# A second TensorE loop, and an earlier start of the first, in a one-core attention decode kernel

## The chip, the cores and the metric

One core of one Trainium2 chip runs the whole kernel. The metric is device time in microseconds (us), the median of several executions. The record marks all runs reported here as fast.

## The reference, cut to what matters

Two attention decode steps (one query per sequence, batch 4, 32 heads of 128) are computed and put side by side. Part A is a sliding window: 8 key/value heads, of whose cache only the last 2048 positions count. Part B is full: 32 heads, 8192 positions.

```python
# A: W = 2048, keys and values repeated 4 times over the query heads
q = (x @ wq) per head;  s = q . k[:, :, -W:] * Dh**-0.5;  o = softmax(s) . v[:, :, -W:];  a = o @ wo
# B: the same with all 8192 positions and no repetition
return concatenate([a, b], axis=-1)
```

587 MB are read once (587.21 MB in the trace of before, at 426 GB/s over the span, with the DMA engines over 90% busy in all but the last of its forty slices): this is a kernel of memory traffic.

## The kernel before

The work is cut into *chunks*. A has 8 (one key/value head, all four sequences; 2 MB of keys and 2 MB of values). B has 128 (two heads of one sequence; 4 MB and 4 MB); I number them 8 to 135. For each chunk TensorE transposes the keys in groups of 8 tiles into PSUM; VectorE and ScalarE copy the groups out (`kt`), TensorE multiplies them with the query (`sc`), the other engines do the softmax, and TensorE multiplies the values (`po`) one chunk later, between the groups of the next.

```python
def keys_part(c):                        # transposes of chunk c, scores two groups behind
    if c >= NCA and (c - NCA) % 2 == 0:
        sch.mark()                       # a loop round may start here: pairs of B chunks only
    for g in range(ch["NG"]):
        emit_T(ch["s"] + g)
        if g >= SLAG: emit_S(ch["s"] + g - SLAG)
        ...                              # statistics of chunk c-1, in A also its exp and sums
for c in range(NC):
    keys_part(c)
    ...
    values_part(c - 1 if c else None, c) # values of chunk c-1, last scores and row maxima of c
```

A recording layer keeps each engine's instructions with the semaphore counts that they wait for. `periods` finds the longest stretch that repeats with constant steps, and only that becomes a hardware loop; the rest is written out. Before, the loops of TensorE, VectorE and ScalarE run from the second pair of B (chunk 10) to the end.

SBUF holds ten half-slots of 2 MB. B uses two slots of two halves each for keys and two for values. A key slot is free when the chunk's last transpose is done, a value slot when its `po` product is done; only then does the SP queue issue the next load into it, strictly in order (in the trace of after B's first keys go out at 112.02 us, behind output weights that waited for their slot until 111.05).

```python
HALF_A = {"k": (2, 3, 8, 0, 1), "v": (6, 7, 9, 4, 5)}     # A: five half-slots each
at = HALF_A[kind][c % 5] if ch["ab"] == 0 else (0 if kind == "k" else 4) + 2 * (c % 2)
waits = take((kind, c), at, ..., ("T", ch["s_last"]) if kind == "k" else ("pv", c))
```

Of the kernel before, what the change touches and what calls it, by code (L numbers as in the profile page):

```python
# [12 lines left out]
P = 128  # L13
# [4 lines left out]
NWO = 3  # L18
# [25 lines left out]
class _Sched:  # L44
# [39 lines left out]
    def emit_ops(self, ops, eng, sems, step=None, count=None):  # L84

        waited = {}
        for k, (emit, waits, sig, at) in enumerate(ops):
            for sname, val in self.needs(waits).items():
                if waited.get(sname, 0) >= val:
                    continue  # L90
                by = step[sname] if step else 0
                eng.wait_ge(sems[sname], count * by + val if by else val)
                waited[sname] = val
            if at is None:
                ins = emit(eng)
            else:
                ins = emit(eng, count * step[k] if step else 0)
            if sig is not None:
                ins.then_inc(sems[sig[0]], sig[1])
# [4 lines left out]
    def periods(self, engname, pairs):  # L104


        ops, marks = self.ops[engname], [m[engname] for m in self.marks]
        rec = _Record()
        says = [(emit(rec) if at is None else emit(rec, -at), sig) for emit, _, sig, at in ops]
        best = (0, 0, {})  # L110
        for a in range(len(marks) - pairs):
            w0, w1 = marks[a], marks[a + pairs]
            n, step = 1, {}
            while a + (n + 1) * pairs < len(marks):
                v0, v1 = marks[a + n * pairs], marks[a + (n + 1) * pairs]
                fine = says[w0:w1] == says[v0:v1]
                for k in range(w1 - w0 if fine else 0):
                    x, y = self.needs(ops[w0 + k][1]), self.needs(ops[v0 + k][1])
                    if ops[w0 + k][3] is not None:
                        x[k], y[k] = ops[w0 + k][3], ops[v0 + k][3]  # L120
                    fine = fine and set(x) == set(y)
                    for c in set(x) & set(y):
                        fine = fine and y[c] - x[c] == n * step.setdefault(c, (y[c] - x[c]) // n)
                if not fine:
                    break
                n += 1
            if n > best[1]:
                best = (a, n, step)
        return best

    def emit_looped(self, engname, eng, sems, loop, pairs):

        a, n, step = self.periods(engname, pairs)
        assert n > 2 and all(v >= 0 for v in step.values()), (engname, a, n, step)
        ops, m = self.ops[engname], [x[engname] for x in self.marks]
        self.emit_ops(ops[:m[a]], eng, sems)
        with loop(0, n) as i:
            self.emit_ops(ops[m[a]:m[a + pairs]], eng, sems, step, i)
        self.emit_ops(ops[m[a + n * pairs]:], eng, sems)


def bass_concat_heads__sliding_block_cached__mha_block_cached__decode_kernel(
# [10 lines left out]
    assert B_wq.shape[1] // P == HQ == HB and HQ % 4 == 0  # L153
# [31 lines left out]

    sch = _Sched()
    with ExitStack() as es:
# [70 lines left out]
        HALF_A = {"k": (2, 3, 8, 0, 1), "v": (6, 7, 9, 4, 5)}  # L258
# [33 lines left out]
        def dma_kv(kind, c):  # L292
            ch = chunks[c]
            T = {("k", 0): A_k, ("k", 1): B_k, ("v", 0): A_v, ("v", 1): B_v}[(kind, ch["ab"])]

            at = HALF_A[kind][c % 5] if ch["ab"] == 0 else (0 if kind == "k" else 4) + 2 * (c % 2)

            if kind == "v" and c == NC - 1:
                at = 8
            waits = take((kind, c), at, 1 if ch["ab"] == 0 else 2, ("T", ch["s_last"]) if kind == "k" else ("pv", c))  # L300
            if ch["ab"] == 0:
                src = T[:, ch["g"], SkA - W:, :].rearrange("b (pp j) d -> pp b (j d)", pp=P // NB)
                sch.add_dma("sp", lambda e: e.dma_start(kv[:, at, :], src), "d_h%d" % at, waits=waits, key=(kind, c))
                return
            src = T[ch["b"], 2 * ch["hp"]:2 * ch["hp"] + 2].rearrange("u (pp j) d -> (u pp) (j d)", pp=P // 2)
            dst = flat(at, 2)
            if kind == "v" and c == NC - 1:

                j0 = 0
                for i, n in enumerate(LASTV):  # L310
                    x = slice(j0 * P, (j0 + n) * P)
                    sch.add_dma("sp", lambda e, x=x: e.dma_start(dst[:, x], src[:, x]), "d_vl%d" % i, waits=waits, key=("vl", j0))
                    j0 += n
                return
            sch.add_dma("sp", lambda e: e.dma_start(dst, src), "d_h%d" % at, waits=waits, key=(kind, c))
# [3 lines left out]
        dma_wq(0, 8)  # L319
        dma_kv("k", 0)  # L320
        dma_wq(1, 4)

        loads = [("k", c + 1) for c in range(NC - 1)]
        for c in range(NC):
            loads.insert(2 * c + 1, ("v", c))
        for kind, c in loads:
            if kind == "k" and c >= NCA and (c - NCA) % 4 == 3:
                dma_wos((c - NCA) // 4)
            dma_kv(kind, c)
            if kind == "v" and c > NCA + 2 and (c - NCA) % 2 == 1:  # L330

                sch.add("sp", lambda e: e.sem_inc(sems["eng_sp"], 1), waits=[("wos", (c - NCA - 2) // 4)], key=("wos2", c - 2), self_inc=True)
            if kind == "v" and c < NCA:
                dma_wo(c)
# [55 lines left out]
        def emit_T(s):  # L390
            c, g = groups[s]
            bank = g % NTRB
            before, bank_used[bank] = bank_used[bank], s
# [17 lines left out]
        def emit_qb(c):  # L411

            col = NB * HQ + 2 * (c - NCA)
            sch.add("dve", lambda e, x=0: e.tensor_copy(qb[:, c % 2, 0:2], qs[:, bass.ds(x + col, 2)]), at=col,
                    waits=["c_qb", ("S", chunks[c - 2]["s_last"])] if c - 2 >= NCA else ["c_qb", ("q", 1)], key=("qb", c))

        def emit_S(s):
            c, g = groups[s]
            ch = chunks[c]
            for t in range(TG):  # L420
# [7 lines left out]
                q = qb[:, c % 2, 0:n] if ch["ab"] == 1 else qs[:, 16 * ch["g"]:16 * ch["g"] + n]  # L428
                waits = []
                if t == 0:  # L430
                    waits = [("ev", s)] + sc_read[bank]
                    if g == 0:
                        waits += [("qb", c) if ch["ab"] == 1 else ("q", 0)]
                    sc_read[bank] = []
# [51 lines left out]
        def stats_exp(c):  # L486
# [8 lines left out]
            pw = [("c_pb", ab)] + ([("pv", prev)] if prev >= (0 if ab == 0 else NCA) else [])  # L495
# [33 lines left out]
        def emit_pv(c, g):  # L529
            ch = chunks[c]  # L530
# [15 lines left out]
        def norm_sum(c):  # L546
            if chunks[c]["ab"] == 0:
                m, n, rs, ri = c % NSM, 16, rst[0][:, c % NSM, :], rinv[:, c % NSM, :]
            else:
                m, n, rs, ri = NSM, 4, rst[1][:, :], rinv[:, 0, 0:4]  # L550
# [12 lines left out]
        def norm_out(c):  # L563
            if chunks[c]["ab"] == 0:
# [6 lines left out]
            waits = [("rinv" if c < NCA else "rz", c), ("pv", c)] + ([("fin", c - 2)] if c >= 2 else [])  # L571
# [3 lines left out]
        def emit_fin(c):  # L575
            ch = chunks[c]
            ab = ch["ab"]
# [11 lines left out]
            for i, (l, r) in enumerate(ops):  # L589
                pe_mm(fin[p0:p0 + NB, :], l, r, start=i == 0 and c == 0, stop=i == len(ops) - 1 and c == lastc,  # L590
                      waits=waits if i == 0 else [], key=("fin", c) if i == len(ops) - 1 else None)
# [10 lines left out]

        def keys_part(c):
            ch = chunks[c]
            if c >= NCA and (c - NCA) % 2 == 0:
                sch.mark()
            for g in range(ch["NG"]):
# [4 lines left out]
                if 1 <= c <= NCA and g == 2:  # L612
                    stats_gmax(c - 1)
                if 1 <= c <= NCA and g == 3:
                    stats_exp(c - 1)
                if 1 <= c <= NCA and g == 6:
                    norm_sum(c - 1)
                if 2 <= c <= NCA + 1 and g == 4:
                    emit_fin(c - 2)
                if c > NCA + 1 and (c - NCA) % 2 == 0 and g == 6:  # L620
                    norm_sum(c - 1)
                if c > NCA + 2 and (c - NCA) % 2 == 1 and g == 10:
                    emit_fin(c - 2)

        def values_part(c, nxt):
# [7 lines left out]
            if nxt + 1 < NC and nxt + 1 >= NCA:  # L633
# [8 lines left out]
            for g in range(16):  # L642
                if c is not None and g < chunks[c]["NG"]:
                    emit_pv(c, g)
                    if g == chunks[c]["NG"] - 1:
# [3 lines left out]

        emit_xT()  # L650
        emit_q(0)
        for c in range(NC):
            keys_part(c)
            if c == 0:
                emit_q(1)

                pe_mm(fin[0:NB, :], qb[:, 0, 0:NB], pbt[0][:, 1, 0:DO], stop=False, waits=["c_qb", ("c_pb", 0)])
            values_part(c - 1 if c else None, c)
# [21 lines left out]
        def _(e):  # L680
            sch.emit_looped("pe", e, sems, loop_on(mybir.EngineType.PE, 0), 1)

        @block.vector
        def _(e):
            sch.emit_looped("dve", e, sems, loop_on(mybir.EngineType.DVE, 0), 1)

        @block.scalar
        def _(e):
            sch.emit_looped("act", e, sems, loop_on(mybir.EngineType.Activation, 0), 1)
# [31 lines left out]
```

## Time and profile before

| | before |
|---|---|
| median, lowest, highest (us) | 1383.21, 1381.66, 1383.74 |
| profiled run (us), its span in the trace | 1381.51, 1379.4 |
| TensorE busy, VectorE, ScalarE | 85%, 46%, 32% |
| DMA, mean over the span | 426 GB/s |
| instructions fetched on TensorE's queue | 27 packets, 0.44 MB |

How to read it: the DMA share is full in every stretch and the rate in B is 431 GB/s, while no compute engine is full. So the time is set by the DMA engines, and a compute engine matters where it makes the DMA queue wait. In this trace the issues of the B keys for chunks 10, 11 and 12 stand as follows (timeline of the SP queue; columns are start and duration in us, then the issue):

```profile
133.08 0.33 SPq L315 DMA_DIRECT2D kv<-in_B_k_cache_dram  x1
148.96 0.33 SPq L315 DMA_DIRECT2D kv<-in_B_k_cache_dram  x1
171.09 0.33 SPq L315 DMA_DIRECT2D kv<-in_B_k_cache_dram  x1
```

Each is some 23 to 28 us ahead of its landing, of which 9.7 us are the transfer itself (4.19 MB at the 431 GB/s of B, an estimate): the queue always has something behind the load in progress.

### The profile page before, as it was taken

Reading aid. Unit: us, or ns where it says so; the run is one execution under the profiler, and the core shown is the slowest. Engines: PE = TensorE matmul, PEld = TensorE weight load, DVE = VectorE, ACT = ScalarE, POOL = GpSimd, SP = SyncE. Lnnn points to the kernel's source line nnn. Section 1 sums busy time; section 2 is a strip of 40 time slices with the busy share of each in tenths; the row PEclk is TensorE's granted clock in tenths of the full one; section 3 lists DMA queues with packets and bytes.
Section 4 is the critical chain, followed back from the end, with each engine's and each line's share of the span. In section 5 each row is a group of like instructions: output and inputs, shape, how many; then the busy total and the mean of one; then the engine's idle time right before and its main releaser. Section 6 shows DMA issues by size and latency. Waiting matters only on the chain.

```text
span 1379.4 us, 58812 instructions
## 1 busy us (share of the span) xinstructions
PE 1172.3 (85%) x26769; PEld 1130.3 (82%) x26769; DVE 639.2 (46%) x1326; ACT 435.9 (32%) x649; POOL 4.5 (0%) x16
## 2 busy tenths in 40 slices
PE   4887889898889888888898888888998889888988
PEld 4767878897879888887888888888888888788887
DVE  1665444444445444444444444444444444444444
ACT  1554323332333322332333222322333233223322
POOL 1000000000000000000000000000000000000000
PEclk9999999999999999999999999999999999999999
DMA  9999999999999999999999999999999999999997
GB/s 400 415 415 426 424 430 430 429 434 428 435 428 434 430 429 429 430 437 426 436 430 430 429 430 436 425 437 430 431 430 429 433 428 436 429 433 430 429 432 311
DMA packets 30097, 587.72 MB, mean 426 GB/s; under 512 B 2784, under 2 KB 10992, under 8 KB 11248
## 3 DMA queue, kind: packets, MB, share of 16 engines
q1 hardware_dynamic: 30040, 587.22, 99.6%
q8 instruction: 27, 0.44, 0.1%
q14 instruction: 6, 0.05, 0.0%
q10 hardware_dynamic: 24, 0.01, 0.0%
HBM read 587.21 MB, written 0.01 MB: 426 GB/s over the span
## 4 chain that ended last, share of the span: by engine, by line
DMA 61%; PE 36%; DVE 1%; issue 1%; ACT 0%; SPq 0%; ACTq 0%; DVEq 0%
DMA kv<-in_B_k_cache_dram 59%; PE tr L344 22%; PE sc L346 9%; DMA kv<-in_B_wq_dram 2%; PE po L346 2%; PE fin L346 2%; PE ms L346 1%; DVE sA L453 1%; DVE kt L406 0%; DVE rm L462 0%; DVE sA L451 0%; ACT pba L516 0%; PE ms L344 0%; ACT kt L404 0%; DVE outsb L593 0%
## 5 line engine op out<-in xcount | busy, mean ns | idle before, releaser
L344 PE MATMUL tr<-identb,kv 128*128 128x128 bf16 x8704 | 704.4, 232 | 172.4 <-DMA kv<-in_B_k_cache_dram 162.2
L406 DVE COPY kt<-tr 128x1024 bf16<-128x1024 bf16 x736 | 502.7, 691 | 480.7 <-PE tr L344 480.4
L344 PEld LDWEIGHTS tr<-identb,kv 128*128 128x128 bf16 x8704 | 559.6, 105 | 197.5 <-DMA kv<-in_B_k_cache_dram 118.1
L404 ACT ACTIVATE kt<-tr 128x1024 bf16<-128x1024 bf16 x352 | 360.2, 1024 | 636.0 <-PE tr L344 632.5
L346 PE MATMUL sc<-qb,kt 128*128 128x64 bf16 x8192 | 424.8, 197 | 0.7 <-issue 0.5
L346 PEld LDWEIGHTS sc<-qb,kt 128*128 128x128 bf16 x8192 | 351.2, 101 | 3.0 <-issue 0.6
L346 PE MATMUL po<-pbb,kv 128*128 128x64 bf16 (+1 forms) x8192 | 289.3, 191 | 6.5 <-issue 6.5
L346 PEld LDWEIGHTS po<-pbb,kv 128*128 128x128 bf16 x8192 | 262.8, 97 | 8.6 <-issue 6.8
L501 ACT ACTIVATE pbb<-sc,negb 64x128 bf16<-64x128 f32 x128 | 51.2, 400 | 294.9 <-DVE negb L491 294.1
L467 DVE TENSOR_REDUCE rm<-sc 64x1 f32<-64x128 f32 x128 | 37.0, 289 | 92.8 <-PE sc L346 91.9
L479 DVE TENSOR_REDUCE gm<-ms 1x2 f32<-1x128 f32 (+1 forms) x72 | 20.0, 278 | 44.2 <-PE ms L344 44.2
L491 DVE COPY negb<-ms 128x1 f32<-128x1 f32 (+1 forms) x72 | 11.4, 159 | 55.3 <-PE ms L346 55.3
L346 PE MATMUL sc<-qs,kt 128*128 128x64 bf16 (+3 forms) x512 | 25.8, 195 | 6.1 <-DVE kt L406 5.8
L346 PE MATMUL ms<-identf,gx 1*128 1x1 f32 (+1 forms) x144 | 27.2, 256 | 1.0 <-DVE gx L483 1.0
L346 PEld LDWEIGHTS sc<-qs,kt 128*128 128x128 bf16 x512 | 20.7, 100 | 8.7 <-DVE kt L406 6.9
L346 PEld LDWEIGHTS ms<-identf,gx 1*128 1x128 f32 (+1 forms) x144 | 21.0, 182 | 5.3 <-DVE gx L483 1.4
L501 ACT ACTIVATION_READ_ACCUMULATOR pbb<-sc,negb 64x1 f32 x128 | 23.7, 185 | 0.0
L344 PE MATMUL ms<-identf,rm 128*1 128x128 f32 (+1 forms) x72 | 19.5, 271 | 0.2 <-DVE rm L467 0.2
L346 PE MATMUL fin<-wos,oz 128*4 128x512 bf16 x64 | 19.4, 385 | 0.3 <-DVE oz L572 0.3
L346 PE MATMUL po<-pba,kv 128*128 128x64 bf16 x512 | 19.0, 193 | 0.3 <-issue 0.3
L483 DVE TENSOR_SCALAR gx<-gm 1x128 f32<-1x128 f32 (+1 forms) x72 | 15.9, 221 | 2.5
L346 PEld LDWEIGHTS po<-pba,kv 128*128 128x128 bf16 x512 | 16.6, 98 | 0.3 <-issue 0.3
(47 smaller groups left out, 146.1 us busy)
## 6 DMA issues: line engine op xcount, KB each, us to landing
kv<-in_B_k_cache_dram SPq DMA_DIRECT2D x64, 4096.0 KB, 27.0
kv<-in_B_v_cache_dram SPq DMA_DIRECT2D x63, 4096.0 KB, 31.7
kv<-in_A_k_cache_dram SPq DMA_DIRECT2D x8, 2048.0 KB, 28.8
kv<-in_A_v_cache_dram SPq DMA_DIRECT2D x8, 2048.0 KB, 26.4
kv<-in_A_wq_dram SPq DMA_DIRECT2D x1, 4096.0 KB, 12.5
kv<-in_B_wq_dram SPq DMA_DIRECT2D x1, 4096.0 KB, 27.0
wor<-in_A_wo_dram SPq DMA_DIRECT2D x8, 512.0 KB, 25.3
wos<-in_B_wo_dram SPq DMA_DIRECT2D x16, 256.0 KB, 20.5
```

The lines of the kernel that those rows point to most:

```text
L344: sch.add("pe", lambda e: e.transpose(o, l, r), waits, key)
L346: sch.add("pe", lambda e: e.matmul(o, l, r, start=start, stop=stop), waits, key)
L404: sch.add("act", lambda e: e.activation(dst, src, ACTF.Copy), waits=waits, key=("ev", s))
L406: sch.add("dve", lambda e: e.tensor_copy(dst, src), waits=waits, key=("ev", s))
L453: emit = lambda e, src=src, b=b: e.scalar_tensor_tensor(out=t, in0=src, scalar=mk[:, b:b + 1], in1=t, op0=ALU.mult, op1=ALU.add)
L467: sch.add("dve", lambda e, src=src, pp=pp: e.tensor_reduce(out=rm[pp, m, 0:1], in_=src, axis=AX.X, op=ALU.max), waits=[("S", ch["s_last"]) ...
L479: sch.add("dve", lambda e: e.tensor_reduce(out=gm[0:C, m, 0:U], in_=src, axis=AX.X, op=ALU.max), waits=[("trm", c)], key=("gmax", c))
L483: sch.add("dve", lambda e: e.tensor_scalar(out=dst, in0=gv, scalar1=-scale, scalar2=None, op0=ALU.mult), waits=[("gmax", c)], key=("gx", c))
L491: sch.add("dve", lambda e: e.tensor_copy(negb[:, m, 0:C], ms[:, col:col + C]), waits=[("bc", c)], key=("negb", c))
L501: sch.add("act", lambda e, src=src, pp=pp, n=n, u=u: e.activation(pbv[pp, :, u], src, ACTF.Exp, bias=negb[pp, m, 0:1], scale=scale, accum_ ...
```

## The change

The intent is a shorter program: TensorE's part of A becomes a loop over pairs too, and B's loop takes in its first pair. For that, everything that differed between rounds must become equal: A gets two half-slots each for keys and values and two for output weights; A's query goes through the small buffer `qb` as B's does; A's last chunk is finished before B starts instead of between B's groups; its values are therefore loaded before B's first keys; and in B's first pair the work for the chunk that does not exist (values and output of "chunk -1") is done on zeros.

```diff
-NWO = 3
+NWO = 2
-        HALF_A = {"k": (2, 3, 8, 0, 1), "v": (6, 7, 9, 4, 5)}
+        HALF_A = {"k": (8, 9), "v": (6, 7)}
-        dma_wq(0, 8)
+        dma_wq(0, 0)
...
+        loads.remove(("v", NCA - 1))
+        loads.insert(loads.index(("k", NCA)), ("v", NCA - 1))
...
         def emit_pv(c, g):
+            if c == NONE:
+                for t in range(TG):
+                    j = g * TG + t
+                    pe_mm(po[:, 2:2 + NW], flat(6, 2)[:, j * P:(j + 1) * P], pbt[1][:, 1, 2 * j:2 * j + NW], ...)
...
-            if c >= NCA and (c - NCA) % 2 == 0:
+            if c % 2 == 0:
                 sch.mark()
...
+        def finish_A():
+            stats_gmax(NCA - 1); emit_fin(NCA - 2); stats_exp(NCA - 1); norm_sum(NCA - 1)
+            for g in range(chunks[NCA - 1]["NG"]): emit_pv(NCA - 1, g)
+            pv_done(NCA - 1); emit_fin(NCA - 1)
...
         for c in range(NC):
+            if c == NCA:
+                sch.mark()
+                finish_A()
             keys_part(c)
-            values_part(c - 1 if c else None, c)
+            values_part(None if c == 0 else NONE if c == NCA else c - 1, c)
```

`finish_A` is joined into fewer lines here. `periods` becomes `runs`, which finds several stretches and lets the first round of one wait for less than the later ones. On VectorE and ScalarE no round of A repeats and B's first pair differs (memsets instead of products), so their loops still start at chunk 10.

## The prediction

> **What bounds the kernel now.** I read the page's forty slices first, then busy time and rate by stage (the windows view), then the chain that ended last, then the timelines of TensorE and of the SP queue around the hand-over from the sliding-block part (A) to the block-cached part (B). The slices:
>
> ```profile
> DMA  9999999999999999999999999999999999999997
> GB/s 400 415 415 426 424 430 430 429 434 428 435 428 434 430 429 429 430 437 426 436 430 430 429 430 436 425 437 430 431 430 429 433 428 436 429 433 430 429 432 311
> HBM read 587.21 MB, written 0.01 MB: 426 GB/s over the span
> ```
>
> The DMA engines have no hole from the first slice to the last; only the rate differs, about 415 GB/s in A (slices 1 to 3) and 430 in B. The stages (columns: window, its length, busy time of PE, weight loads, DVE, ACT, POOL with counts, granted clock, DMA share, GB/s):
>
> ```profile
> 40.00:120.00 80.00, 62.85 (x1337) 54.70 (x1335) 46.98 (x114) 40.14 (x61) 0.00 (x0) 0.97 1.02 417
> 200.00:1340.00 1140.00, 985.50 (x22627) 958.37 (x22628) 528.29 (x1078) 351.64 (x527) 0.00 (x0) 0.93 1.00 431
> ```
>
> In both stages DMA is full and TensorE is not (79% and 86%). So the time is bytes over rate, plus a tail of about 22 us after the last key chunk has landed (the chain shows that landing at 1355.06 us in a span of 1379.4). Compute matters only if it holds a buffer so long that the DMA queue runs dry. A microsecond of empty queue is lost for good; a microsecond of TensorE delay is not. The timeline of TensorE shows that A itself has almost no compute slack:
>
> ```profile
> 56.65 1.51 PE L344 MATMUL tr<-identb,kv 128*128 128x128 bf16 x24
> 67.89 1.51 PE L344 MATMUL tr<-identb,kv 128*128 128x128 bf16 x24 [0.29 <-DMA kv<-in_A_k_cache_dram]
> 79.52 1.51 PE L344 MATMUL tr<-identb,kv 128*128 128x128 bf16 x24 [0.83 <-DMA kv<-in_A_k_cache_dram]
> 91.74 1.51 PE L344 MATMUL tr<-identb,kv 128*128 128x128 bf16 x24 [1.96 <-DMA kv<-in_A_k_cache_dram]
> 103.46 1.51 PE L344 MATMUL tr<-identb,kv 128*128 128x128 bf16 x24 [2.02 <-DMA kv<-in_A_k_cache_dram]
> ```
>
> Each line is the first transposes of one A chunk. A chunk takes 11.1 us of compute (45.41 to 56.65, less 0.1); its 4.72 MB (keys, values, a block of the output weights) take 11.3 us at 417 GB/s, and 11.7 to 12.2 between the later lines. TensorE rides on the landings, and gains 0.3 to 1 us a chunk when it is behind. The entry of the existing loop, two chunks into B:
>
> ```profile
> 154.14 0.41 PE L346 MATMUL po<-pbb,kv 128*128 128x64 bf16 x8
> 158.14 2.74 PE L344 MATMUL tr<-identb,kv 128*128 128x128 bf16 x24 [3.60 <-issue]
> 171.88 0.73 PE L346 MATMUL po<-pbb,kv 128*128 128x64 bf16 x19 [0.44 <-issue]
> 179.06 0.35 PE L346 MATMUL po<-pbb,kv 128*128 128x64 bf16 x6 [3.24 <-issue]
> 199.00 0.79 PE L346 MATMUL po<-pbb,kv 128*128 128x64 bf16 x21 [2.81 <-issue]
> ```
>
> Here the last loads had landed (the chain puts the key landing at 156.23), yet TensorE waits for nothing the profile shows. Between 171.88 and 179.06 stand 124 matmuls, about 248 instructions with the weight loads. I find no such waits from 200 to 500 us, in the later rounds of the loop. I read them as instructions arriving for the first time.
>
> [...]instruction queue 27 packets and 0.44 MB (16 KB each), and stalls some 250 instructions apart.[...] 24 transposes take 2.74 us after the 3.60 us hole and 1.51 otherwise; with the slower groups after them a hole costs about 2 us more.[...]The first load here takes 12.5 us for 4.19 MB, where 431 GB/s would give 9.7[...].
>
> **The change, part by part.**
>
> *Code.* The instruction order shows that only TensorE gets the second loop (chunks 2 to 7 of A, three rounds); its B loop now has all 32 rounds of pairs. Its program falls from 3466 to 2057 entries. Of 0.44 MB of instructions perhaps 0.18 is no longer fetched: 0.18 MB at 430 GB/s is **0.4 us of DMA saved**.
>
> *Added work.* 128 zero matmuls for the absent chunk (35 ns each, from 289.3 us over 8192: 4.5 us), two memsets, a short copy of the queries per A chunk (about 0.16 us on DVE). All beside DMA; no direct cost.
>
> *Buffers.* A's keys and values get two half-slots each instead of five, output weights two instead of three. Let a key chunk of A land at k. The queue then carries values, weights, the next keys (landing k+11.3), values, weights; the keys that reuse this slot have their turn at k+17.6. Their release, the last transpose, is 8.4 us after the chunk starts (45.41 to 53.8). [...]**TensorE may lag by about 7 us in A** before the queue runs dry. The value slot (9 us) and the weights, released at the output matmul 6.3 us into a later chunk (8 us), bind less. Before, the lag is under 1 us. So the five slots weren't needed at this lag; half the prefetch costs nothing by itself.
>
> *First jump.* At 45.4 us the new A loop is entered. [...]So a hole of 4 to 5 us, and 2 us of slow clock; against that the usual 1.5 us wait for DVE in that place falls away. Lag about 5.5 us: under 7. It shrinks with each chunk to about 3 at chunk 7.
>
> *Hand-over.* The last A values are now loaded before the first B keys: 2.1 + 0.52 + 0.26 MB, 6.8 us at 425 GB/s, so these keys land at 119.42 + 6.8 = 126.2. No bytes are added. In the meantime TensorE finishes A serially: chunk 7 starts at 106.3, its scores are out 11 us later, row maximum at 119, the statistics and exp to about 124 (1.7 us of ACT copies among them), 64 matmuls and the projection to about 127.8. Then the jump into the B loop: fetched by about **131, a lag of 5 us**. Before, this finishing lay between B's own groups.
>
> *First round of B.* The same stalls as in the trace above now fall in the first pair: from one chunk start to the next it took 21.8 us (158.14 to 179.90) and 20.4 (to 200.28), then 17. So starts at 131.3, 153.1, 173.5, 190.5; keys land at 126.2, 136 (now directly behind), 155.5, 175. The keys' reload is issued 13.3 us after the first start and 12.4 after the later ones: at 144.6, 165.5, 185.8; the turns are 145.8, 165.3, 184.8. [...]**About 3 to 4 us of DMA lost.** Later TensorE gains 2.5 us a chunk and the steady slack returns.
>
> *Sum.* 1383.2 − 0.4 + 3.3, less about 0.6 because A's tail may be shorter than I made it: **1385.5 us**.
>
> **The rivals.** *All hidden:* the lag at the B entry is 2 us less than I think (the jump's fetch passes while A's statistics run). Nothing then runs dry, and the saved fetch gives 1382.8. For it: the turns are missed by under 2 us, near my error. *The A loop starves the queue:* further fetch holes in the first A round[...] carry the lag past 7 us; then two-deep slots hold the queue in each A chunk, 2 to 3 us over three or four chunks: 1390 to 1393. Against it: straight code ran through A with only 0.25 us of such a hole[...]. *Less code frees DMA or TensorE noticeably:* the queue's share is 0.1%, so at most 1.4 us if all of it vanished: 1382. TensorE as the bound is excluded by its 14% of idle time in B.
>
> **Range and chances.** The three runs of before spread by 2 us. The hidden case sets the lower end, 1382.0; starvation in A the upper, 1391.0. Two per cent is 27.7 us: to be slower by that the queue would have to run dry by 3.5 us at each of A's eight chunks; to be faster, bytes or the rate would have to change. So faster 0.01, same 0.97, slower 0.02.
>
> **What would show it.** Right: rate and DMA share in B unchanged at 431 and 1.00; instruction bytes near 0.26 MB; an "issue" hole of 4 to 5 us near 45 us; in A waits for keys at the chunk starts gone or shrunk; first B keys used at about 131 with a hole before them; a dip in DMA share between 140 and 190 us worth 3 us and none after. Wrong: a DMA share under 0.97 in 40 to 120 us (the rival of A), no dip at all (hidden), or another rate or tail in B. A result outside 1375 to 1395 would mean that I missed a wait, most likely one of the SP queue, which issues in order and so passes any late release on to every load behind it.

- *Sum.* It came to 1385.5 us, with 3.3 us of lost DMA work. That term was worked out with a latency between issue and landing. The trace of before gives 2.8 us for the first load (12.5 us less 9.7). With it the issues at 144.6, 165.5 and 185.8 miss their turns by 1.6, 1.4 and 0.8 us, each counted beyond what those before it have shifted: 3.8 us, and a sum of 1386.0 (an estimate from the prediction's own times). The lag of 7 us in A had the latency taken off too; 17.6 less 8.4 less 2.8 leaves 6.4.
- *Jumps.* The hole of 4 to 5 us at the first and the fetch up to 131 us at the second were estimates of how instructions arrive, not shown. Measured is this: from one to the next of the holes at 158.14, 171.88, 179.06 and 199.00 us the windows view of before counts 495, 252 and 749 matmuls and weight loads (those across a bound included).
- *Rivals and range.* Why straight code has only the one hole of 0.25 us in A (at 112.31), and that the 431 GB/s of B could not rise, was not shown.

## The result, and the profile after

| | before | after |
|---|---|---|
| median (us), 6 runs each | 1383.08 | 1385.8 |
| lowest to highest | 1381.45 to 1384.34 | 1384.74 to 1388.13 |
| ratio | | 1.0023, 95% interval 1.001 to 1.0036 |
| profiled run | 1381.51 | 1388.13 |
| instruction bytes, TensorE's queue | 0.44 MB | 0.26 MB |

A ratio is the mean time of one kernel's fast runs over that of the other's of the same rounds, so it is not the ratio of the medians; redone from the single runs, the ratios of the experiments come out only if the profiled run is left out of them. The change costs 0.2%, clear of noise: "same" by the 2% measure, slower by 2.7 us in fact. Mind that the profiled run of after is its slowest; its trace shows the mechanism larger than a median run has it.

The slices of the page after (compare the rows at the head of the prediction):

```profile
DMA  9999989999999999999999999999999999999997
GB/s 400 414 416 410 424 351 429 431 436 429 428 431 434 427 432 433 428 432 430 431 427 436 430 427 436 430 428 429 436 430 427 436 430 427 430 436 429 428 431 320
HBM read 587.21 MB, written 0.01 MB: 424 GB/s over the span
```

The sixth slice (173 to 208 us) has fallen to 351 GB/s, the only DMA share under 9 before the end. From the seventh on the rate is that of before. The windows view in 20 us stretches, before and then after, columns as in the prediction:

```profile
180.00:200.00 20.00, 17.20 (x384) 16.53 (x379) 8.95 (x17) 5.98 (x9) 0.00 (x0) 0.91 0.99 424
```

```profile
180.00:200.00 20.00, 20.00 (x467) 19.86 (x465) 11.18 (x23) 7.59 (x11) 0.00 (x0) 0.93 0.70 285
```

(424 - 285) / 424 of 20 us is 6.6 us of DMA work that was not done. Within it, after, in 2 us stretches:

```profile
182.00:184.00 2.00, 2.00 (x37) 2.00 (x36) 1.43 (x4) 0.09 (x1) 0.00 (x0) 0.78 0.72 311
184.00:186.00 2.00, 2.00 (x51) 2.00 (x49) 1.33 (x3) 1.02 (x1) 0.00 (x0) 1.00 0.08 33
186.00:188.00 2.00, 2.00 (x51) 2.00 (x49) 1.33 (x3) 1.02 (x1) 0.00 (x0) 1.00 0.00 0
188.00:190.00 2.00, 2.00 (x63) 2.00 (x61) 1.03 (x2) 1.02 (x1) 0.00 (x0) 1.00 0.25 66
```

The queue is simply empty until 189 us, while TensorE runs without a pause. What it waits for is in the SP queue of after, the issues of the keys for chunks 10, 11 and 12:

```profile
139.70 0.33 SPq L334 DMA_DIRECT2D kv<-in_B_k_cache_dram  x1
161.41 0.33 SPq L334 DMA_DIRECT2D kv<-in_B_k_cache_dram  x1
189.00 0.33 SPq L334 DMA_DIRECT2D kv<-in_B_k_cache_dram  x1
```

The third comes 18 us later than its counterpart of before, when the last transpose of chunk 10 is done; everything issued earlier had landed by 186.7 us. Why TensorE was so late with chunk 10 is in its timeline (first transposes of A's first loop round, then of chunk 8, then the holes):

```profile
46.23 1.51 PE L367 MATMUL tr<-identb,kv 128*128 128x128 bf16 x24 [0.21 <-DVE sA L480]
...
128.87 1.51 PE L367 MATMUL tr<-identb,kv 128*128 128x128 bf16 x24
...
147.11 0.37 PE L369 MATMUL po<-pbb,kv 128*128 128x64 bf16 x7 [2.44 <-issue]
...
168.52 0.80 PE L369 MATMUL po<-pbb,kv 128*128 128x64 bf16 x22 [3.45 <-issue]
...
177.01 0.61 PE L369 MATMUL sc<-qb,kt 128*128 128x64 bf16 x8 [4.16 <-DVE kt L431]
```

Three things are to be seen. The entry of A's loop at 46 us has no instruction hole at all. In B's first pair the holes "issue" are where the prediction put them (2.44 and 3.45 us, and two of 0.7). And there is one it did not have: TensorE stands 4.16 us for VectorE in chunk 10, because VectorE itself stands, before the first copy of its loop (timeline of VectorE after, then of before at the same place):

```profile
176.26 1.29 DVE L431 COPY kt<-tr 128x1024 bf16<-128x1024 bf16 x2 [6.16 <-issue]
```

```profile
159.21 0.69 DVE L406 COPY kt<-tr 128x1024 bf16<-128x1024 bf16 x1 [4.73 <-PE tr L344]
```

Before, VectorE entered its loop at the same chunk, but TensorE and the keys were not there either (it waits for `tr`), so the same entry was hidden. After, TensorE's own first-time holes have moved two chunks forward and VectorE's comes after them: they add up instead of lying upon each other. TensorE's granted clock then stays at 0.50 from 176.1 to 182.9 us, so eight transposes take 1.04 us instead of 0.61, and chunk 10 takes 23.6 us from start to start where 17 had been usual.

That "issue" stands for instructions still under way is a reading of the packets of the instruction queues: TensorE's long holes end 1.3 and 1.6 us after a packet of 16 KB has landed (at 145.8 and 166.9 us), VectorE's 1.8 us after one of 8 KB (at 174.5).

To say how much DMA work is lost, I add up the bytes of all packets in the trace up to a given time, subtract from the same sum in before's trace, and divide by 431 GB/s. In after's profiled run this deficit is 0 at 100 us, 1.5 us at 120, 1.1 at 180, 7.6 at 200, and 7.5 from there to 1340 us. So two losses and nothing else: 1.5 us at the end of A and 6.5 us at chunk 12's keys. The first is a wait of the SP queue too (views of after; the last line is the same block's issue in before):

```profile
109.15 1.87 PE L369 MATMUL fin<-wor,oT 128*4 128x512 bf16 x4
111.05 0.37 SPq L300 DMA_DIRECT2D wor<-in_A_wo_dram  x1
```

```profile
96.67 0.37 SPq L283 DMA_DIRECT2D wor<-in_A_wo_dram  x1
```

It is the last block of A's output weights that waits, 7.2 us, for its slot (now one of two instead of three), until chunk 5's output product ends; B's first keys, which the old order had ahead of it, stand behind it and are issued at 112.02.

The span is longer by 6.6 us, not by 7.5. One more count explains that. The trace has 16 landing times for each load, which I read as those of the 16 DMA engines' shares, and TensorE waits for the last: of the last chunk's keys in before the first share landed at 1348.51 us and the last at 1355.01, and TensorE began on them at 1355.06 (in after 1358.15, 1360.06 and 1360.10). The *spread* between first and last engine tells how far the slowest is behind:

| spread (us) of loads landing by | 60 us | 140 us | 220 us | 1000 us | the last |
|---|---|---|---|---|---|
| before | 2.0 | 3.7 | 6.6 | 6.5 | 6.4 |
| after | 2.1 | 2.2 | 0.5 | 1.9 | 1.8 |

In before the spread grows from 2.0 to 6.6 us while instructions are fetched (25 of the 27 packets of TensorE's queue come before 198 us) and then stands still. The hole of after evened it out, from 3.3 us at the load that landed at 186.7 us to 0.5 at the next, 201.2: the early engines idled longer. Part of after's lost 7.5 us was therefore time in which the early engines would only have run ahead. The last load landed at 1379.6 us against 1374.6, 5.0 us later; the remaining 1.6 us are in the tail, where TensorE began the last chunk on its slow clock (granted clock 0.62 in 1360 to 1362 us, 0.53 in the next two; from the chain of waits, after, then before):

```profile
1360.10 2.44 PE tr L367 x24
```

```profile
1355.06 1.51 PE tr L344 x24
```

### The profile page after: what moved, and what is told of

Its sections match the earlier page's. It is cut to its first block, busy times and chain, and to the rows that moved or that the text cites. A ratio compares the mean times of both kernels' runs of the same rounds, so it can differ in the third digit from the quotient of the medians.

```text
span 1386.0 us, 59254 instructions
## 1 busy us (share of the span) xinstructions
PE 1181.4 (85%) x26901; PEld 1137.5 (82%) x26901; DVE 640.3 (46%) x1337; ACT 436.2 (31%) x649; POOL 4.5 (0%) x16
## 4 chain that ended last, share of the span: by engine, by line
DMA 59%; PE 37%; DVE 2%; issue 1%; ACT 0%; SPq 0%; ACTq 0%; DVEq 0%
DMA kv<-in_B_k_cache_dram 57%; PE tr L367 21%; PE sc L369 10%; PE po L369 3%; PE fin L369 2%; DMA kv<-in_B_wq_dram 2%; DVE sA L482 1%; PE ms L369 1%; DVE kt L431 0%; DVE rm L491 0%; DVE sA L480 0%; ACT pba L545 0%; PE ms L367 0%; DVE outsb L640 0%; ACT kt L429 0%
## 5 line engine op out<-in xcount | busy, mean ns | idle before, releaser
L369 PE MATMUL sc<-qb,kt 128*128 128x64 bf16 x8704 | 449.6, 197 | 15.7 <-DVE kt L431 15.4
L369 PEld LDWEIGHTS sc<-qb,kt 128*128 128x128 bf16 x8704 | 371.5, 101 | 19.8 <-DVE kt L431 17.2
L369 PE MATMUL po<-pbb,kv 128*128 128x64 bf16 (+1 forms) x8320 | 293.9, 191 | 6.6 <-issue 6.6
L369 PEld LDWEIGHTS po<-pbb,kv 128*128 128x128 bf16 x8320 | 267.0, 97 | 8.6 <-issue 6.9
L508 DVE TENSOR_REDUCE gm<-ms 1x2 f32<-1x128 f32 (+1 forms) x72 | 20.1, 279 | 44.5 <-PE ms L367 44.4
L369 PE MATMUL ms<-xT,kv 128*128 128x4 bf16 x256 | 7.1, 166 | 8.6 <-DMA kv<-in_A_wq_dram 4.4
L369 PEld LDWEIGHTS ms<-xT,kv 128*128 128x128 bf16 x256 | 7.0, 104 | 8.8 <-DMA kv<-in_A_wq_dram 4.5
```

The source lines that it names most:

```text
L369: sch.add("pe", lambda e: e.matmul(o, l, r, start=start, stop=stop), waits, key)
L508: sch.add("dve", lambda e: e.tensor_reduce(out=gm[0:C, m, 0:U], in_=src, axis=AX.X, op=ALU.max), waits=[("trm", c)], key=("gmax", c))
```

## The experiments

Theory 1: TensorE comes late into B and loses more by instruction holes of its own and of VectorE, so that the key slot for chunk 12 (sometimes 11) is freed after the DMA queue has run dry. Rivals: theory 2, the shallow buffers of A; the A loop itself; the load order; a loss that is not in the queue. Each kernel ran five rounds beside the kernel before, whose median was 1383.1 to 1383.4 us in each set. All gave correct results.

**Depth of A's buffers alone** (kernel before):

```diff
-NWO = 3
+NWO = 2
-        HALF_A = {"k": (2, 3, 8, 0, 1), "v": (6, 7, 9, 4, 5)}
+        HALF_A = {"k": (8, 9), "v": (6, 7)}
-        dma_wq(0, 8); dma_wq(1, 4)
+        dma_wq(0, 0); dma_wq(1, 2)
```

> The kernel before with only the buffers of the change: two half-slots each for A's keys and values, two for its output weights, and the changed places of the two query weights. If the loss of the change comes from TensorE reaching the first chunks of B late (theory 1), this kernel is as fast as before, 1383 us within 1, and the DMA share from 40 to 120 us stays at 1.0. If the shallow buffers starve the queue in A (theory 2), it is slower by 2 us or more, with a dip of the DMA share before 120 us.

Measured: 1381.75 us, ratio 0.9994 (0.9981 to 1.0007). The window where A ends:

```profile
100.00:120.00 20.00, 13.12 (x302) 11.58 (x300) 10.17 (x26) 7.49 (x11) 0.00 (x0) 0.98 1.01 421
```

The DMA share stays at 1.01. The shallower buffers suffice in A with the old load order, and there theory 2 falls. With the new order it was not tested, and the third output-weight slot was given back in no run.

**A straight again on TensorE, B's loop as changed:**

```diff
-        for first, n, a, step in self.runs(engname):
+        for first, n, a, step in [r for r in self.runs(engname) if r[1] > 8]:
```

> The changed kernel with its A part straight again on TensorE (the loop over B keeps all 32 rounds). Theory 1: the A loop costs nothing, since the trace shows no hole at its entry; 1385.8 us within 1, the hole in the DMA share around 180 to 190 us stays, and the instruction bytes rise from 0.26 MB by about 0.1 MB. If the A loop itself is the cost, the time falls to 1383.

Measured: 1385.28 us, ratio 1.0026 (1.0012 to 1.004): no better than the change. The A loop costs nothing. The instruction bytes are 0.36 MB, as expected. Its profiled run took 1385.0 us, near the median of the change, so it shows the usual size of the hole: VectorE stands 5.52 us at its loop entry, and

```profile
180.00:200.00 20.00, 20.00 (x490) 19.37 (x488) 11.68 (x23) 8.08 (x11) 0.00 (x0) 1.00 0.86 356
```

The deficit of bytes is 0.3 us at 180 us and 4.1 at 200.

**B's first pair written out on TensorE:**

```diff
-            if n > 2 and a > 0 and self.moved(...)
+            if n > 2 and a > 0 and False and self.moved(...)
```

> The changed kernel with the first pair of B written out on TensorE, zero work included, so that its loop starts at the second pair, as the loops of VectorE and ScalarE do. Theory 1 (first-time instruction holes of TensorE in the first pair, then that of VectorE at the second, add up to more lag than a key slot allows): the holes of TensorE in chunks 8 and 9 go, the lag at chunk 10 is under 8 us, and the queue no longer runs dry; 1383 us within 1. If the serial end of A or the load order is what counts, it stays at 1385 to 1386.

Measured: 1382.83 us, ratio 1.0003 (0.9989 to 1.0016). The loss is gone in the mean, though the interval overlaps that of the change. And the runs scatter: 1381.6, 1381.7 and 1381.9 on one side, 1383.8, 1386.4 and 1387.8 on the other. The profiled run is one of the slow ones (1386.4), and there the hole is at the end of A:

```profile
100.00:120.00 20.00, 16.38 (x335) 13.74 (x332) 11.34 (x28) 9.91 (x16) 0.00 (x0) 0.91 0.86 336
```

(416 - 336) / 416 of 20 us are 3.8 us; from 140 to 200 us the share is 1.00 or 1.01. TensorE's holes in chunks 8 and 9, which were expected to go, only shrank (1.21, 1.37, 0.72 and 2.43 us). With the first pair out of the loop the hole in B is gone but for about 1 us after 200 us, though in this run the earlier hole had already moved the loads. That earlier one, at the end of A, is occasional. There the queue waits again for the slot of A's last output weights, whose issue comes at 113.04 us; from 112 to 114 us the DMA share is 0.02. The profiled runs with the new order sort by this issue: at 108.01 to 109.36 us (four runs) there is no such dip, at 110.63, 111.05 and 113.04 there is. In these three the output product took 1.87 us, at a granted clock of 0.50 to 0.60, instead of 1.03. Chunk 7 also began later in this run (105.33 us, against 101.8 to 103.5 in the others). What decides, no run tests.

**VectorE without its loop:**

```diff
-            sch.emit_looped("dve", e, sems, loop_on(mybir.EngineType.DVE, 0))
+            sch.emit("dve", e, sems)
```

> The changed kernel with VectorE's program written out in full, without its loop. Theory 1: the 6.1 us hole before VectorE's first eviction of chunk 10 goes, TensorE's wait of 4.2 us for it too, the keys of chunk 12 are issued 4 to 5 us earlier and the DMA share of 180 to 190 us rises from 0.41 to over 0.8; 1383.5 to 1384.5 us. If VectorE's entry does not matter (some other wait takes its place), the hole stays and the time is 1385.8.

Measured: 1385.03 us, ratio 1.0019 (1.0006 to 1.0032). Half a miss. The hole did go:

```profile
180.00:200.00 20.00, 20.00 (x520) 19.37 (x518) 10.99 (x23) 7.05 (x10) 0.00 (x0) 1.00 0.97 411
```

The byte deficit is 0.7 us at 200 us and still only 0.8 at 1340. Yet the profiled run took 1387.6 us. The spread of the engines tells why: 1.9 us at 300 us, 3.3 at 600, 6.3 at 1000, 8.2 at the end, with a single engine out of line and the other fifteen within 1.9 us. From 277 to 1232 us the trace has eight instruction packets of 8 KB more than after's, one every 137 us or so, on the queue that brings VectorE's instructions among others (q14). (8.2 - 1.9) / 8 is **0.8 us of one engine for each packet** (the packet itself shows as 0.33 us), and they all fall on the same engine, or the other fifteen would not stay within 1.9 us. The last chunk's keys were late for want of that one engine's share:

```profile
1359.07 2.74 PE L367 MATMUL tr<-identb,kv 128*128 128x128 bf16 x24 [4.50 <-DMA kv<-in_B_k_cache_dram]
```

This asked for a test by itself.

**The kernel before without VectorE's loop:**

```diff
-            sch.emit_looped("dve", e, sems, loop_on(mybir.EngineType.DVE, 0), 1)
+            sch.emit("dve", e, sems)
```

> The kernel before with VectorE's program written out in full. It settles why the changed kernel without VectorE's loop had no hole and still was not faster: in its trace nine more instruction packets of 8 KB came from 277 to 1232 us, and the spread between the first and the last of the 16 DMA engines to finish a load grew from 1.9 to 8.2 us. If each such packet holds up one engine of the 16 and always the same one (theory 3), this kernel is slower by 3 to 6 us with no hole in its DMA share and with a spread of over 10 us at the end. If an instruction packet costs only its bytes, some 80 KB at 430 GB/s, it is slower by 0.2 us, within the noise of before.

Measured: 1386.22 us, ratio 1.0023 (1.0009 to 1.0036). No hole (byte deficit 0.2 us at 1340), spread 6.7 us at 220 us and 10.4 at the end. The time is just under the expected range, the spread as expected (it counted nine packets; the ninth, between 463 and 470 us, is in most versions). Some 64 KB of extra instructions cost 2.9 us, not 0.2. (The spread grows by 3.7 us, less than eight times 0.8; it would if the engine that they hit was not the latest at first, which was not shown.)

**A delay of TensorE at the start of B,** in the changed kernel and in the one before:

```diff
             emit_fin(NCA - 1)
+            for j in range(128):
+                pe_mm(po[:, 256:256 + NW], identb[:, :], pbt[1][:, 1, 0:NW])
```

> The changed kernel with 128 matmuls of no use (28 ns each, about 3.6 us) after the end of A, just before TensorE enters B. Theory 1 (TensorE's lateness at the start of B empties the DMA queue in the first four chunks, so there is no slack left there): nearly all of it is paid, 1388 to 1389.5 us, with a wider hole in the DMA share between 140 and 200 us. If the loss of the change sits elsewhere (A's buffers, fetches, the tail), B's start has slack and the time stays at 1385.8 within 0.5.

Measured: 1387.65 us, ratio 1.0029 (1.0016 to 1.0043). Slower than the change, 1.9 us by the medians and 0.8 by the ratios, but not by nearly all of the 3.6 us, and the intervals overlap: a miss in size. (In the trace the matmuls take 3.91 us, and the loop's entry after them has an instruction hole of 1.69 that the change does not have.) In B the queue now falls short in three stretches instead of one, the third 180 to 200 us at 0.90:

```profile
140.00:160.00 20.00, 16.50 (x347) 16.19 (x345) 7.78 (x17) 5.00 (x8) 0.00 (x0) 0.83 0.89 360
160.00:180.00 20.00, 14.34 (x353) 13.60 (x351) 7.50 (x16) 6.03 (x9) 0.00 (x0) 0.91 0.91 375
```

The byte deficit is 9.0 us at 200 us. A load that is held up earlier also has its followers' turns moved back, so the delays need not simply add; and the spread at the end is 2.0 us.

> The kernel before with the same 128 matmuls of no use before its second chunk of B. Theory 1: the lag there is under 5 us and a key slot allows about 15, so nothing is paid: 1383 us within 1 and no hole in the DMA share. If any delay of TensorE costs time (TensorE bound in some hidden way), 1386 to 1387.

(The 15 us are an estimate: before's B keys were issued 23 to 28 us ahead of their landing, less the 9.7 of the transfer, 13 to 18.) Here the same 128 matmuls (on A's probability buffer) stand before chunk 9. Measured: 1383.1 us, ratio 0.9997 (0.9984 to 1.0011), byte deficit 0.1 us. Chunk 10 starts at 165.40 us instead of 158.14, and nothing is paid. The kernel before has the slack that the change has used up.

**Key loads of B in halves,** each half freed and awaited by itself, in both kernels:

```diff
+            if kind == "k":
+                for i in range(2):
+                    w = take((kind, c, i), at + i, 1, ("T", ch["s"] + 7 + 8 * i))
+                    x = slice(i * 8192, (i + 1) * 8192)
+                    sch.add_dma("sp", lambda e, x=x: e.dma_start(dst[:, x], src[:, x]), ..., waits=w, key=(kind, c, i))
```

> The changed kernel with each key chunk of B loaded as two DMAs of 2 MB, each half freed as soon as its own half of the transposes is done and each half awaited by itself. Theory 1: the first half is asked for some 5.5 us earlier and the second has its turn 4.9 us later, so the queue does not run dry between 140 and 200 us, worth 3 us or more; TensorE also starts the last chunk on its first half, some 4 us sooner at the end. Together 1377 to 1379 us, which would beat both kernels. If key slots are not what runs out, only the end gains: 1381 to 1382.

Measured: 1384.3 us, ratio 1.0017 (1.0003 to 1.003). The hole is gone, although VectorE still stands 6.02 us at its loop entry and TensorE 5.37 for it; but the rate of the long middle has fallen:

```profile
180.00:200.00 20.00, 20.00 (x494) 19.37 (x491) 11.82 (x23) 8.15 (x12) 0.00 (x0) 1.00 1.00 421
...
260.00:1300.00 1040.00, 895.49 (x20549) 866.96 (x20547) 476.02 (x977) 318.30 (x476) 0.00 (x0) 0.93 1.01 429
```

The byte deficit is 0.3 us at 200 us, but grows from 0.6 at 300 to 4.6 at 1340: some 53 chunks with one more DMA each, about 0.075 us for each. So key slots are what runs out, and the expected time was missed because with key loads of 2 MB the rate is 429 GB/s from 260 to 1300 us, against the 431 of B with 4 MB, which I had left out.

> The kernel before with the same halved key loads. It had no hole in its queue, so it shows what the end alone gains: about 4 us, 1378.5 to 1380. The changed kernel with halves should then be as fast or up to 2 us faster, as it fetches fewer instructions; if it is still 2 to 3 us slower, the loss of the change is not in the key slots.

Measured: 1386.62 us, ratio 1.0024 (1.001 to 1.0038): slower than before by the same falling rate (byte deficit 5.0 us at 1340). The gain at the end that I expected did not show. With this cost in both kernels and the hole in neither, the changed one is 2.3 us *faster* by the medians, 1.3 by the means of the runs; the intervals overlap. Its spread at the last load is 3.5 us against 6.7.

**The old load order at the hand-over,** in the changed kernel:

```diff
-        loads.remove(("v", NCA - 1))
-        loads.insert(loads.index(("k", NCA)), ("v", NCA - 1))
```

> The changed kernel with the loads at the hand-over in the order of before: the first keys of B ahead of A's last values. Theory 1: these keys are there before TensorE can use them in either order, so TensorE enters B no earlier, perhaps 1 us later as A's last values land at about 124 us; the hole around 180 to 190 us stays and the time is 1385 to 1386.5, though the dip of 110 to 120 us goes. If the load order is what costs, 1383.

Measured: 1387.38 us (1383.37 to 1388.69), ratio 1.0031 (1.0018 to 1.0045). That is above the expected range; the order is not the cost of the hole in B. TensorE enters B at 128.35 us, hardly earlier, and the hole stays even in the profiled run, the fastest of the five:

```profile
180.00:200.00 20.00, 20.00 (x492) 19.37 (x490) 11.96 (x23) 8.08 (x11) 0.00 (x0) 1.00 0.89 369
```

The dip of 110 to 120 us is gone (421 GB/s from 100 to 120): the output weights are issued at 109.07 us, but B's first keys went ahead of them, at 98.89.

**Both undone: old load order, and B's first pair written out:**

> The changed kernel with both undone: the load order of before, and B's first pair written out on TensorE. The run with the pair alone written out was at 1381.6 to 1381.9 in half of its runs and 1384 to 1388 in the others, whose profile shows a hole at 110 to 120 us, where A's last values wait for a slot. Theory 1: with another load in between that hole goes too; 1381 to 1383 in all runs, at or a little below the time of before. If the scatter comes from elsewhere, it stays.

Measured: 1384.33 us, ratio 1.0006 (0.9992 to 1.0019), four runs at 1383.9 to 1384.6 and one, the profiled, at 1387.1. Not as expected: the hole at the end of A is gone (with the output weights issued at 110.86 us, late enough for a dip in the other order), but the profiled run has one in B again:

```profile
200.00:220.00 20.00, 16.77 (x367) 15.94 (x364) 8.11 (x16) 5.86 (x9) 0.00 (x0) 0.91 0.90 367
```

TensorE's holes now stand in chunks 10 and 11 (the longest 4.09 us), with the lateness from the serial end of A before them. The margin is thin in all versions that finish A first. This run is inconclusive on the scatter.

**VectorE's loop entered three pairs later,** the rest as changed:

```diff
+            first, n = first + late, n - late          # late = 3 for VectorE, 0 for the others
             self.emit_ops(ops[done:m[first]], eng, sems)
```

> The changed kernel with VectorE's loop over B entered three pairs later (at chunk 16, near 290 us) and the pairs before written out, at a cost of one or two more instruction packets of 8 KB. It tests what the run without VectorE's loop left mixed: the gain from taking VectorE's entry away from chunk 10, and the loss from the long program's packets. Theory 1 and 3: TensorE's own holes in chunks 8 and 9 stay, VectorE's moves to where TensorE is no longer late, so there is at most 1 us of hole in the DMA share between 140 and 200 us and none near 290; with the few packets of the change the spread of the engines stays near 2 to 4 us; 1381 to 1383 us, as fast as before or a little faster. If VectorE's entry is not what empties the queue, 1385 to 1386.

Measured: 1381.77 us (1380.52 to 1383.57), ratio to before 0.9994 (0.9981 to 1.0008), against 1.0023 (1.001 to 1.0036) of the change: the intervals do not overlap. Three rounds of VectorE's loop are written out, and the whole loss is gone. The window of the former hole:

```profile
180.00:200.00 20.00, 20.00 (x518) 19.29 (x515) 10.25 (x24) 6.18 (x10) 0.00 (x0) 1.00 1.01 434
```

VectorE's entry costs the same 5.5 us where it stands now, two packets of 8 KB moved with it (from 174.2 and 180.0 us to 274.6 and 280.4), and nobody pays for it:

```profile
276.69 1.29 DVE L432 COPY kt<-tr 128x1024 bf16<-128x1024 bf16 x2 [5.47 <-issue]
```

TensorE's holes of 2.44 and 3.18 us in chunks 8 and 9 are still there, as is the late entry (125.86 us). The byte deficit at 1340 us is -0.2. The profiled run is 1.0 us shorter than before's, the median 1.4 us under before's; the interval includes "equal", so it is at least as fast as before, and no version is shown to beat it.

## Why the prediction was right or wrong

The time (1385.5 predicted, 1385.8 measured), the class and the place of the loss were right. Point by point:

- *What bounds the kernel, and that compute counts only where it empties the queue:* right. The rate in B is 431 GB/s in both; adding 3.6 us to TensorE's work is free before (0.9997); after, it cost 1.9 us by the medians, with overlapping intervals. The 7.6 us of DMA work that after lacked at 200 us were still 7.5 at 1340: the queue did not make them up.
- *Buffers:* right for A by itself (0.9994), wrong at the hand-over. The prediction let the output weights bear a lag of 8 us and called the keys what binds. With B's keys moved behind them their turn comes earlier, at the landing of A's last values (113.2 us), and they were issued at 111.05. The load that was issued to an empty queue landed about 2.5 us later than its transfer takes (estimate: keys of chunk 12, 189.00 to 201.2 us, less 9.7), so the weights bound first.
- *First jump:* wrong. No hole of 4 to 5 us at 45 us: the wait is 0.21 us, for VectorE, and writing A out again changes nothing. A packet of 16 KB had landed at 44.5 us, as one had at 43.8 in before's straight code. The lag of 5.5 us through A that was built on it did not exist either.
- *Hand-over:* nearly right. B's first keys landed at 127.0 us (126.2 predicted); TensorE was in B at 128.87 instead of 131, in other runs at 125.9 to 131.3, since the second jump did not stall here either. (With the delay before B it did, 1.69 us at 134.43; before's entry at 158.14 stood 3.60, though the keys landed only at 156.2. Why an entry stands in one place and not in another no run shows.)
- *First round of B:* the mechanism was right, the sizes were not. Predicted starts of chunks 8 to 11: 131.3, 153.1, 173.5, 190.5; in the profiled run 128.87, 147.96, 170.18, 193.78. The predicted three near misses became two loads in time (issued at 139.70 and 161.41) and one that was late by far (189.00 against 185.8). The mis-sized term is chunk 10: I had taken its 17 us from before, where VectorE's loop entry lay under another wait. Uncovered, it is a hole of 5.5 to 6.3 us for VectorE and 4.2 to 5.7 us for TensorE where B's first pair is in the loop, and in after 5.9 us at the slow clock follow. (How long a hole brings the slow clock the runs do not settle: 24 transposes took 2.74 us in before after waits of 1.32 and 3.60 us, at 18.25 and 158.14, and 2.75 us soon after one of 2.17, without VectorE's loop; they took 1.51 after waits of 2.02, at 103.46, and 1.69, with the delay before B.) The sum came out right partly by luck: this missing term was made up for by the jump stalls that did not occur. That moving VectorE's entry alone recovers the whole loss shows how much hung on it.
- *Code:* the bytes were right (0.26 MB), their worth was not. I spread 0.18 MB over 16 engines and got 0.4 us. Without VectorE's loop each packet of 8 KB cost one engine 0.8 us (an estimate, from the spread of 8.2 us less 1.9), and a load waits for the slowest, as the last chunk's keys show (1355.01 us, its first share 1348.51). The spread at the end of a hole-free run of the changed code is 3.4 us (VectorE's loop late) against 6.4 of before, and that run beats before's by 1.0 us; the halved versions differ by 1.3 to 2.3 us. So it may be worth 1 to 2 us (an estimate); no interval shows it alone.
- *Tail:* the 22 us are 24.3 by the prediction's own two numbers (1379.4 less 1355.06); nothing rests on it.
- *Rivals:* "all hidden" and "the A loop starves the queue" are both refuted, the first by the hole, the second by the runs on depth and on A's loop. What I did not foresee is the occasional hole at the end of A, 1.5 us in after's profiled run. The traces show what the queue waits for there, the slot of the last output weights with B's keys behind it. Why TensorE is late with it in some runs only stays open.

## What to carry to other kernels

In a kernel bound by DMA, count for each buffer how late its release may be, and then add up all delays that can fall into one stretch, on every engine: an instruction hole that cost nothing while it lay under another wait is uncovered when that wait moves (here VectorE's, 6.16 us in after). Where first-time code must be fetched, let the engines enter their loops in different, slack places (VectorE three pairs later: 1381.77 us, against 1385.8). When the order of loads changes, work out each buffer's margin again: two output-weight slots were enough in one order and not always in the other. And don't charge small fetches at the mean rate of all DMA engines (some 64 KB in packets of 8 KB, under 0.2 us by that rate, cost the kernel before 2.9 us); look at the spread of the 16 engines of a load.
